# Reordering the first microseconds: a strip's part split around a tile's turns, turns and strip parts exchanged, and PSUM emptied by ScalarE for tiles 0 and 2 and by VectorE for tiles 1 and 3

## The chip, the cores and the metric

The kernel runs on one core of a Trainium2 chip. The metric is the device time of one execution in microseconds (us). The kernel before takes 215.81 us (median of 3 runs, 215.74 to 215.83). The change touches only the first 12 us, in which TensorE waits 0.72 us in all (below), so it can only matter by tenths of a microsecond.

## The reference, cut to what matters

```python
x = A_x                                           # 2048 x 640, bf16
g = sigmoid((x * gate_w).sum(-1, keepdims=True))
a = state_space(x, ...)                           # complex diagonal scan, 640 states
b = gelu(x @ w1 + b1) @ w2 + b2                   # w1: 640 x 1728
out = g * a + (1 - g) * b
```

The change concerns only the start of `x @ w1` for the first 512 rows of x (chunk 0).

## The kernel before, the parts that the change touches

TensorE contracts over partitions, so x is needed transposed, as `xT[0][:, k, row]` with k = 0 to 4 counting 128-wide slices of the 640 columns. The later chunks are transposed by DMA. Chunk 0 is needed first and is handled otherwise: its four 128-row tiles are loaded as they are and each 128x128 block is turned on TensorE by a matmul with the identity. A turn lands in PSUM, and VectorE or ScalarE copies it to `xT`. The loads are issued in pieces, in order of urgency:

```python
    load_x0(nc.sync, 0, 1, 0, KA * P)             # tile 0, k = 0 and 1 (KA = 2)
    load_w1a(nc.scalar, 0)
    load_x0(nc.sync, 1, 2, 0, KA * P)             # tile 1
    load_w1a(nc.scalar, 1)
    load_x0(nc.sync, 2, 3, 0, KA * P)             # tile 2
    load_x0(nc.scalar, 0, H, KA * P, D)           # tiles 0 and 1, k = 2 to 4
    load_x0(nc.sync, 3, 4, 0, KA * P)             # tile 3
    load_w1a(nc.sync, 2)
    # ... (cut)
    rows(nc.sync, prmA[0:KS, :], A_log_dt)        # three small parameter loads
    rows(nc.sync, prmA[KS:2 * KS, :], A_Lambda_im)
    rows(nc.sync, prmA[2 * KS:3 * KS, :], A_Lambda_re)
    load_x0(nc.sync, H, TPC, KA * P, D)           # tiles 2 and 3, k = 2 to 4: "the x load"
    nc.sync.dma_start(out=w1a34[:], ...)          # w1 for k = 3 and 4: "the w1 load"
```

Dummy matmuls keep TensorE busy until the first tile is there. Then turns and useful matmuls alternate:

```python
    pA = bank()
    for n in (512, 512, 512, 512, 512, 128, 128, 128, 128):
        nc.tensor.matmul(pA[:, 0:n], lhsT=ones(P), rhs=ones(n), start=True, stop=True)

    def turn(p, col, a, kd):
        nc.tensor.matmul(p[:, col:col + P], lhsT=xn[0][:, a, kd * P:(kd + 1) * P], rhs=ident[:], start=True, stop=True,
                         skip_group_check=True)

    def turned(engine, p, col, a, k0, k1):
        dst = xT[0][:, k0:k1, a * P:(a + 1) * P]
        src = p[:, col:col + (k1 - k0) * P].rearrange("p (k t) -> p k t", t=P)
        if engine is nc.vector:
            nc.vector.tensor_copy(out=dst, in_=src)
        else:
            nc.scalar.activation(out=dst, in_=src, func=ACT.Identity)

    def turn_first(a, other):
        t = bank()
        turn(t, 0, a, 0)
        turned(nc.vector, t, 0, a, 0, 1)
        turn(other, a * P, a, 1)
        turned(nc.scalar, other, a * P, a, 1, 2)

    turn_first(0, pA)
```

Six PSUM banks hold the first six 128-wide slices of the hidden layer for all 512 rows. `part(k, a)` adds slice k of tile a to all six, in six matmuls of 128 columns. `turn_first` turns k = 0 and 1 of a tile, `turn_rest` k = 2 to 4. All eight banks are in use: six accumulators, `pA`, and one that is handed from `bank()` to `bank()`. A turn into a bank must wait until the earlier turn there has been emptied.

```python
    def strip(kd, t0, t1, first, f0=0, f1=FA):
        for kf in range(f0, f1):
            ff1_mm(banks[kf], 0, kf, kd, t0, t1, first, 3)

    def turn_rest(a, t, *parts):
        for k in range(KA, KD):
            turn(t, (k - KA) * P, a, k)
        for engine, k0, k1 in parts:
            turned(engine, t, (k0 - KA) * P, a, k0, k1)

    # ... (cut: scratch tiles and helpers of the state-space part, such as u, red, ab, FSC and over)
    def part(kd, a):
        strip(kd, a * P, (a + 1) * P, kd == 0)

    for _ in range(3):
        nc.tensor.matmul(banks[0][:, 0:P], lhsT=ones(P), rhs=ones(P), start=True, stop=True, skip_group_check=True)
    part(0, 0)
    turn_first(1, pA)
    part(1, 0)
    turn_first(2, pA)
    part(0, 1)
    part(1, 1)
    turn_first(3, pA)
    part(0, 2)
    part(1, 2)
    nc.tensor.matmul(pA[:, 0:3 * KS], lhsT=prmA[:], rhs=ident[:, 0:3 * KS], start=True, stop=True, skip_group_check=True)
    nc.vector.tensor_copy(out=colA[:], in_=pA[:, 0:3 * KS])
    nc.scalar.activation(out=dt16[:], in_=ldt_c, func=ACT.Exp)
    nc.vector.tensor_scalar(out=limp[:], in0=lim_c, scalar1=INV_2PI, scalar2=None, op0=ALU.mult)
    turn_rest(0, bank(), (nc.scalar, KA, KD))
    part(0, 3)
    nc.vector.tensor_tensor(out=dtl[:], in0=dt16[:], in1=lre_c, op=ALU.mult)
    nc.vector.tensor_tensor(out=thp_c[:], in0=dt16[:], in1=limp[:], op=ALU.mult)
    turn_rest(1, pA, (nc.vector, KA, KD))
    nc.scalar.activation(out=r_c[:], in_=dtl[:], func=ACT.Exp)
    part(1, 3)
    turn_rest(2, bank(), (nc.scalar, KA, KD))
    part(2, 0)
    nc.vector.tensor_tensor(out=u, in0=tf[:].rearrange("p (o i) -> p o i", o=1).to_broadcast([P, KS, NP]), in1=over(thp_c[:], NP), op=ALU.mult)
    turn_rest(3, pA, (nc.scalar, KA + 1, KD), (nc.vector, KA, KA + 1))
    nc.vector.tensor_copy(out=kk[:], in_=u)
    nc.vector.tensor_tensor(out=red, in0=u, in1=kk[:], op=ALU.subtract)
    part(2, 1)
    part(2, 2)
    AHEAD = 3
    strip(KD - 1, 0, HT, False, 0, AHEAD)
    part(2, 3)
    nc.scalar.activation(out=FSC[:, 0:KS, 0:NP], in_=red, func=ACT.Sin, scale=TWO_PI_M)
    nc.vector.scalar_tensor_tensor(out=ab, in0=red, scalar=-1.0, in1=red, op0=ALU.mult, op1=ALU.max)
    nc.scalar.activation(out=FSC[:, KS:2 * KS, 0:NP], in_=ab, func=ACT.Sin, scale=-TWO_PI_M, bias=halfpi[:])
    for kf in range(FA):
        if kf == 3:
            nc.tensor.matmul(pA[:, 0:NB], lhsT=prmB[:], rhs=ident[:, 0:NB], start=True, stop=True, skip_group_check=True)
            nc.vector.tensor_copy(out=colB[:], in_=pA[:, 0:NB])
            for j in range(KD):
                nc.vector.tensor_copy(out=w1c[j][:, n1c - 1:n1c], in_=pA[:, j:j + 1])
        for kd in (4, 3):
            ff1_mm(banks[kf], 0, kf, kd, HT if kd == 4 and kf < AHEAD else 0, CH, False, 3)
    for kf in range(FA):
        ff1_act(banks[kf], 0, kf)
    two_banks = [bank(), bank()]
    for kd in range(KD):
        for i in range(2):
            ff1_mm(two_banks[i], 0, FA + i, kd)
    for i in range(2):
        ff1_act(two_banks[i], 0, FA + i)
    ff1(0, FA + 2)
```

## Time and profile before

| | before |
|---|---|
| time, median of 3 runs | 215.81 us |
| span of the profiled execution | 213.8 us |
| TensorE busy | 209.5 us |
| first useful matmul (first strip) | 4.00 us |
| first matmul with `w1b`, the next columns of w1 (end of the part that the change touches) | 12.51 us |
| second half's x load landed / w1 load for k = 3 and 4 landed | 8.16 / 9.14 us |

These lines are from the page of the kernel before: the span, the busy time of two engines with its share of the span, and the chain of work that ended last, by engine and by line.

```profile
span 213.8 us, 3591 instructions
...
PE 209.5 (98%) x1399; PEld 126.2 (59%) x1410; DVE 189.2 (88%) x387; ACT 103.2 (48%) x186; POOL 1.0 (0%) x13
...
PE 95%; DMA 3%; SPq 0%; issue 0%; DVE 0%
PE bank L607 27%; PE bank L267 25%; PE bank L666 20%; PE bank L548 20%; DMA xn<-in_A_x_dram 2%; DMA w1a<-in_B_w_dram 1%; PE bank L623 1%; PE bank L293 1%; SPq L130 0%; PE bank L233 0%; DVE ot L671 0%; PE bank L283 0%; PE bank L395 0%
```

TensorE is the limit, and 3% of the chain are DMAs, all of them in the first 9 us. The next lines are from the timeline of the kernel before, merged into groups: start, duration, engine, line, operation, out<-in, count, and in brackets the idle time just before with what ended it.

```profile
4.00 0.60 PE L267 MATMUL bank<-xT,w1a 128*128 128x128 bf16 x6
...
4.44 0.28 PE L233 MATMUL bank<-ident,xn 128*128 128x128 bf16 x2
...
4.55 0.50 PE L267 MATMUL bank<-xT,w1a 128*128 128x128 bf16 x6
...
4.70 0.29 DVE L240 CAST xT<-bank 128x128 bf16<-128x128 f32 x1 [0.75 <-PE bank L233]
...
5.04 0.27 PE L233 MATMUL bank<-ident,xn 128*128 128x128 bf16 x2
...
5.94 0.83 PE L267 MATMUL bank<-xT,w1a 128*128 128x128 bf16 x12
...
6.92 0.17 PE L368 MATMUL bank<-ident,prmA 128*128 128x15 bf16 x1 [0.15 <-DMA prmA<-in_A_Lambda_re_dram]
...
7.62 0.50 PE L267 MATMUL bank<-xT,w1a 128*128 128x128 bf16 x6
...
8.20 0.17 PEld L233 LDWEIGHTS <-xn 128*128 128x128 bf16 x3 [0.26 <-DMA xn<-in_A_x_dram]
8.20 0.34 PE L233 MATMUL bank<-ident,xn 128*128 128x128 bf16 x3
...
12.51 0.59 PE L267 MATMUL bank<-xT,w1b 128*128 128x512 bf16 x2
```

A merged TensorE line must be read with care: the end of a matmul is modelled and overlaps the next, so a short wait does not appear as a gap. Read starts instead. A 128-column matmul may follow another after 56 ns, so the six of 4.55 us let the next group start at 4.55 + 6 x 0.056 = 4.89 us; it started at 5.04. The 0.15 us are a wait for the VectorE copy on the line before, which began at 4.70, took 0.29 and freed the bank. In the same way, twelve matmuls from 5.94 end their turn at 6.61, and the parameters' turn (L368) started at 6.92; six from 7.62 end at 7.95, and the rest of tile 2 started at 8.20, where the weight load also shows the wait openly, for the x load. These three waits sum to 0.72 us. When a load has landed is read from the semaphore records in the trace, where each of the large loads counts to 16.

### The profile page before, as it was taken

How to read it: one execution, taken by the hardware profiler on the slowest of the kernel's cores; microseconds unless marked ns; L12 is line 12 of the kernel's file. 1: busy time of each engine (PE TensorE's matmuls, PEld its weight loads, DVE VectorE, ACT ScalarE, POOL GpSimd, SP SyncE). 2: the span in 40 equal slices, each digit the busy share in tenths (PEclk: the TensorE clock that was granted, in tenths of full speed). 3: DMA queues.
4: the chain of work that ended last, by engine and by line, in shares of the span. 5: the costliest groups of instructions: out<-in, count | busy, mean ns of one | idle time of the engine just before them, and what ended most of it. 6: DMA issues, size and time to landing. Idle time of an engine off the chain costs nothing.

```text
span 213.8 us, 3591 instructions
## 1 busy us (share of the span) xinstructions
PE 209.5 (98%) x1399; PEld 126.2 (59%) x1410; DVE 189.2 (88%) x387; ACT 103.2 (48%) x186; POOL 1.0 (0%) x13
## 2 busy tenths in 40 slices
PE   8999999999999999999999999999999999999994
PEld 5845444454476644775457777444457687676774
DVE  2699999999998999999999999999999999993153
ACT  3699856675758588203563210455683422305100
POOL 1000000000000000000000000000000000000000
DMA  6879999997000000051000005100000000100011
GB/s 194 247 162 180 208 175 293 312 214 187 0 0 0 3 0 0 17 175 71 0 0 3 0 0 180 68 0 2 3 0 14 3 0 31 61 34 0 0 66 61
DMA packets 31571, 15.84 MB, mean 74 GB/s; under 512 B 22978, under 2 KB 31554, under 8 KB 31554
## 3 DMA queue, kind: packets, MB, share of 16 engines
q1 hardware_dynamic: 30850, 14.99, 28.9%
q10 hardware_dynamic: 704, 0.62, 0.9%
q8 instruction: 11, 0.18, 0.3%
q14 instruction: 6, 0.05, 0.1%
HBM read 7.48 MB, written 2.62 MB: 47 GB/s over the span
## 4 chain that ended last, share of the span: by engine, by line
PE 95%; DMA 3%; SPq 0%; issue 0%; DVE 0%
PE bank L607 27%; PE bank L267 25%; PE bank L666 20%; PE bank L548 20%; DMA xn<-in_A_x_dram 2%; DMA w1a<-in_B_w_dram 1%; PE bank L623 1%; PE bank L293 1%; SPq L130 0%; PE bank L233 0%; DVE ot L671 0%; PE bank L283 0%; PE bank L395 0%
## 5 line engine op out<-in xcount | busy, mean ns | idle before, releaser
L607 PE MATMUL bank<-w_sb,gel 128*128 128x384 bf16 (+1 forms) x416 | 57.9, 299 | 0.0
L607 PEld LDWEIGHTS <-gel 128*128 128x128 bf16 x416 | 40.3, 98 | 17.0 <-issue 0.8
L551 ACT ACTIVATE bu<-bank 128x512 bf16<-128x512 f32 x40 | 23.7, 598 | 37.6 <-PE bank L548 37.5
L272 ACT ACTIVATE gel<-bank,colB 128x512 bf16<-128x512 f32 x52 | 33.8, 694 | 10.9 <-PE bank L267 10.6
L666 PEld LDWEIGHTS <-hs 128*128 128x128 bf16 x330 | 31.7, 98 | 11.6
L502 DVE TENSOR_TENSOR_SCAN g<-r_c,carry,v 128x512 bf16<-128x512 f32 x30 | 37.2, 1269 | 0.0
L615 ACT ACTIVATE gb<-bank,gcol 128x384 f32<-128x384 f32 (+1 forms) x32 | 15.1, 526 | 33.2 <-PE bank L607 16.8
L267 PE MATMUL bank<-xT,w1a 128*128 128x512 bf16 (+2 forms) x173 | 27.7, 310 | 0.2
L666 PE MATMUL bank<-CT_im,hs 128*128 128x320 bf16 (+2 forms) x165 | 27.1, 295 | 0.0
L666 PE MATMUL bank<-CT_re,hs 128*128 128x320 bf16 (+2 forms) x165 | 27.1, 295 | 0.0
L671 DVE SCALAR_TENSOR_TENSOR ot<-bank,gcol,gb 128x320 bf16<-128x320 f32 (+2 forms) x33 | 17.4, 532 | 10.0 <-PE bank L666 9.5
L548 PE MATMUL bank<-xT,BT_im 128*128 128x512 bf16 x99 | 24.8, 379 | 0.1
L548 PE MATMUL bank<-xT,BT_re 128*128 128x512 bf16 x97 | 24.5, 379 | 0.2
L267 PEld LDWEIGHTS <-w1a 128*128 128x128 bf16 x177 | 14.6, 98 | 11.5
L267 PE MATMUL bank<-xT,w1b 128*128 128x512 bf16 x80 | 17.9, 379 | 0.0
L548 PEld LDWEIGHTS <-BT_im 128*128 128x128 bf16 x100 | 9.8, 98 | 11.8
L581 DVE TENSOR_TENSOR bank<-xn,Dbc 128x320 f32<-128x320 bf16 (+2 forms) x33 | 14.5, 482 | 2.0 <-ACT gb L615 2.0
L548 PEld LDWEIGHTS <-BT_re 128*128 128x128 bf16 x100 | 9.7, 98 | 11.0
L483 DVE TENSOR_TENSOR v<-wa,wb 128x512 bf16<-128x512 bf16 x40 | 15.2, 420 | 0.6
L596 ACT ACTIVATE bank<-b2bc 128x384 f32<-128x384 bf16 (+1 forms) x24 | 11.7, 526 | 7.6 <-DVE ot L671 7.6
L483 DVE TENSOR_TENSOR wa<-TCOS,g 128x1024 bf16<-128x1024 bf16 x20 | 13.7, 685 | 0.1
L267 PE MATMUL bank<-xT,w1c 128*128 128x512 bf16 x57 | 13.6, 379 | 0.2
(99 smaller groups left out, 166.0 us busy)
## 6 DMA issues: line engine op xcount, KB each, us to landing
out_dram<-ot SPq DMA_DIRECT2D x15, 160.0 KB, 1.8
w_sb<-in_B_w_dram SPq DMA_DIRECT2D x1, 2080.0 KB
xn<-in_A_x_dram SPq DMA_DIRECT2D x3, 640.0 KB
w1b<-in_B_w_dram SPq DMA_DIRECT2D x5, 128.0 KB, 3.6
w1c<-in_B_w_dram SPq DMA_DIRECT2D x5, 112.0 KB, 2.7
w1a<-in_B_w_dram ACTq DMA_DIRECT2D x2, 192.0 KB, 3.1
w1a<-in_B_w_dram SPq DMA_DIRECT2D x1, 384.0 KB, 4.1
xn<-in_A_x_dram SPq DMA_DIRECT2D x4, 64.0 KB, 2.9
```

The source lines that it names most:

```text
L267: nc.tensor.matmul(p[:, t0:t1], lhsT=w, rhs=xT[c][:, kd, t0:t1], start=(kd == 0) if first is None else first, stop=(kd == last), skip_grou ...
L272: nc.scalar.activation(out=gel[c][:, kf, :], in_=p[:, :], func=ACT.Gelu_apprx_tanh, bias=b1_c[:, kf:kf + 1])
L483: nc.vector.tensor_tensor(out=o, in0=a, in1=b, op=op)
L502: nc.vector.tensor_tensor_scan(s["g"][:, ri, :], r_c[:, ks:ks + 1].to_broadcast([P, CH]), s["v"][:, ri, :], init, ALU.mult, ALU.add)
L548: nc.tensor.matmul(p[:], lhsT=BT[ks >= KSA][:, kd, (ks % KSA if ks < KSA else ks - KSA) * P:][:, 0:P], rhs=xT[c][:, kd, :], start=(kd == 0 ...
L551: nc.scalar.activation(out=bu[:, ri, :], in_=p[:], func=ACT.Identity)
L581: dve_now(ck.pe, 0.45, lambda: nc.vector.tensor_tensor(out=p[:, 0:d1 - d0], in0=xn[c][:, a, d0:d1], in1=Dbc[:, d0:d1], op=ALU.mult))
L596: nc.scalar.activation(out=v, in_=src, func=ACT.Identity)
L607: nc.tensor.matmul(p[:, col:col + d1 - d0], lhsT=gel[c][:, kf, a * P:(a + 1) * P], rhs=w2_sb[:, kf, d0:d1], start=False, stop=False, skip_ ...
L615: nc.scalar.activation(out=gbs[ti][:, d0:d1], in_=p[:, col:col + d1 - d0], func=ACT.Identity, scale=gcol[:, 1, ti:ti + 1])
L666: nc.tensor.matmul(p[:, 0:d1 - d0], lhsT=hs[c][:, j, lo:lo + P], rhs=CT[:, j % KS, d0:d1], start=False, stop=(j == 2 * KS - 1), skip_group ...
L671: nc.vector.scalar_tensor_tensor(out=ot[:, d0:d1], in0=p[:, 0:d1 - d0], scalar=gcol[:, 0, ti:ti + 1], in1=gbs[ti][:, d0:d1], op0=ALU.mult, ...
```

## The change

The intent is to fill these waits. Tile 1's turns start in the middle of tile 0's first part, so that its copy is ready earlier; tile 0's rest is turned ahead of the parameters; the turns that need the x load move behind `part(2, 0)` and `part(2, 1)`; ScalarE empties the rest of tiles 0 and 2 and VectorE that of tiles 1 and 3 (new for tile 3 only, which the two had shared), and the k = 4 strip for the first 256 columns is done for all six banks and earlier.

```diff
--- before.py
+++ after.py
@@ -356,8 +356,9 @@
 
     for _ in range(3):
         nc.tensor.matmul(banks[0][:, 0:P], lhsT=ones(P), rhs=ones(P), start=True, stop=True, skip_group_check=True)
-    part(0, 0)
+    strip(0, 0, P, True, 0, FA // 2)
     turn_first(1, pA)
+    strip(0, 0, P, True, FA // 2, FA)
     part(1, 0)
     turn_first(2, pA)
     part(0, 1)
@@ -365,27 +366,27 @@
     turn_first(3, pA)
     part(0, 2)
     part(1, 2)
-    nc.tensor.matmul(pA[:, 0:3 * KS], lhsT=prmA[:], rhs=ident[:, 0:3 * KS], start=True, stop=True, skip_group_check=True)
-    nc.vector.tensor_copy(out=colA[:], in_=pA[:, 0:3 * KS])
+    turn_rest(0, pA, (nc.scalar, KA, KD))
+    pP = bank()
+    nc.tensor.matmul(pP[:, 0:3 * KS], lhsT=prmA[:], rhs=ident[:, 0:3 * KS], start=True, stop=True, skip_group_check=True)
+    nc.vector.tensor_copy(out=colA[:], in_=pP[:, 0:3 * KS])
     nc.scalar.activation(out=dt16[:], in_=ldt_c, func=ACT.Exp)
     nc.vector.tensor_scalar(out=limp[:], in0=lim_c, scalar1=INV_2PI, scalar2=None, op0=ALU.mult)
-    turn_rest(0, bank(), (nc.scalar, KA, KD))
     part(0, 3)
+    turn_rest(1, bank(), (nc.vector, KA, KD))
     nc.vector.tensor_tensor(out=dtl[:], in0=dt16[:], in1=lre_c, op=ALU.mult)
     nc.vector.tensor_tensor(out=thp_c[:], in0=dt16[:], in1=limp[:], op=ALU.mult)
-    turn_rest(1, pA, (nc.vector, KA, KD))
     nc.scalar.activation(out=r_c[:], in_=dtl[:], func=ACT.Exp)
+    nc.vector.tensor_tensor(out=u, in0=tf[:].rearrange("p (o i) -> p o i", o=1).to_broadcast([P, KS, NP]), in1=over(thp_c[:], NP), op=ALU.mult)
     part(1, 3)
-    turn_rest(2, bank(), (nc.scalar, KA, KD))
     part(2, 0)
-    nc.vector.tensor_tensor(out=u, in0=tf[:].rearrange("p (o i) -> p o i", o=1).to_broadcast([P, KS, NP]), in1=over(thp_c[:], NP), op=ALU.mult)
-    turn_rest(3, pA, (nc.scalar, KA + 1, KD), (nc.vector, KA, KA + 1))
+    part(2, 1)
+    turn_rest(2, pA, (nc.scalar, KA, KD))
+    turn_rest(3, bank(), (nc.vector, KA, KD))
     nc.vector.tensor_copy(out=kk[:], in_=u)
     nc.vector.tensor_tensor(out=red, in0=u, in1=kk[:], op=ALU.subtract)
-    part(2, 1)
+    strip(KD - 1, 0, HT, False)
     part(2, 2)
-    AHEAD = 3
-    strip(KD - 1, 0, HT, False, 0, AHEAD)
     part(2, 3)
     nc.scalar.activation(out=FSC[:, 0:KS, 0:NP], in_=red, func=ACT.Sin, scale=TWO_PI_M)
     nc.vector.scalar_tensor_tensor(out=ab, in0=red, scalar=-1.0, in1=red, op0=ALU.mult, op1=ALU.max)
@@ -397,7 +398,7 @@
             for j in range(KD):
                 nc.vector.tensor_copy(out=w1c[j][:, n1c - 1:n1c], in_=pA[:, j:j + 1])
         for kd in (4, 3):
-            ff1_mm(banks[kf], 0, kf, kd, HT if kd == 4 and kf < AHEAD else 0, CH, False, 3)
+            ff1_mm(banks[kf], 0, kf, kd, HT if kd == 4 else 0, CH, False, 3)
     for kf in range(FA):
         ff1_act(banks[kf], 0, kf)
     two_banks = [bank(), bank()]
```

## The prediction

> **What bounds the kernel now.** TensorE: the busy table gives it 209.5 of 213.8 us, the chain of waits 95%. Measuring from matmul start to matmul start, I find no stall after 12.5 us; all the rest is streaming (a 128-column matmul every 56 ns, 256 every 109 ns, 512 every 216 ns, as "TensorE: Matmul & The Clock Gate", Back-to-back issue gap, states for a warm array: N/2.4 + 2.5 ns). So any time saved before 12.5 us passes whole to the end, and nothing else can be saved. Between the first real matmul (4.00) and 12.5 us TensorE stalls three times, 0.72 us in all (timeline):
> - 0.15 us at 5.04: tile 2's turn waits for VectorE to empty tile 1's turn (same bank);
> - 0.31 us at 6.92: the parameter turn waits for its three small loads, the last landing at 6.79;
> - 0.25 us at 8.20: tile 2's rest waits for the x load that lands at 8.16.
>
> **What changes.** Columns streamed are equal; three wide matmuls become six halves (~8 ns). Tile 1's turns start three strip matmuls earlier; tile 0's rest moves ahead of the parameter turn; tiles 2 and 3's rest moves behind parts (2,0) and (2,1); the whole 256-column strip of k=4 moves ahead of parts (2,2) and (2,3). Replay with the durations and landings of the trace:
> - Tile 1's turn at 4.28 instead of 4.44. VectorE's copy (0.29) ends near 4.83, so the 0.15 us stall goes. But tile 3's x lands at 5.77 and its turn already started at 5.82 without slack: the 0.15 us comes back as a wait there.
> - 6.61: tile 0's rest (0.17) fills part of the parameter wait; parameters still at 6.92. Gain 0.17.
> - Tile 1's rest now shares a bank with the parameters and waits for VectorE's copy of them (ends 7.30): +0.06.
> - Part (2,1) now comes right after (2,0) and needs tile 1's rest, emptied by VectorE in 0.56 us (about 7.72 to 8.28): starts 8.33, +0.14.
> - The x load of 8.16 is no longer waited for. Both rests end at 9.00. The k=4 strip then needs the w1 load that lands at 9.14: starts about 9.19, +0.19. Before it was needed at 9.50.
> - From there 6x109 + 12x56 + 6x325 + 30 ns = 3.30 us: end near 12.49 against 12.51.
>
> So stalls of about 0.70 us replace 0.72: the kernel swaps a wait for x at 8.16 with 4.31 us of work behind it for a wait for w1 at 9.14 with 3.30 us behind it. If landings are earlier without the profiler, both chains shorten about equally; perhaps 0.1 to 0.2 us more for the new one if w1's last piece comes early. That is likely: 15 of its 16 semaphore steps are there at 8.41, the last comes 0.73 us later ("DMA: Bandwidth & Descriptors", Why a DMA increments its semaphore by 16: only the full 16 means all data landed; this trace agrees). ScalarE and VectorE move by at most 0.1 us, and the activations' banks have about 0.9 us of slack at 14.7.
>
> **Time.** 215.7 us, 215.35 to 215.95 eight times in ten. Faster by over 2%: 1%; within 2%: 98%; slower by over 2%: 1%.
>
> **Right or wrong in the profile.** No gap before tile 2's turn; a gap to about 5.82 before tile 3's; parameters at 6.92; small gaps before tile 1's rest and part (2,1); k=4 strip starting 0.05 us after its load lands; first w1b matmul at 12.3 to 12.55; everything after it unchanged but shifted.
>
> **What would make it wrong.** Loads landing at other times (x of tile 3, parameters, last w1 piece), which now decide more; a stall on VectorE before part (2,1) longer than 0.2 us; a different chip.

## The result, and the profile after

| | before | after |
|---|---|---|
| time, median of 6 runs | 215.82 us (215.72 to 215.97) | 215.87 us (215.40 to 216.01) |
| span of the profiled execution | 213.8 us | 214.1 us |
| first strip matmul | 4.00 us | 3.97 us |
| first `w1b` matmul | 12.51 us | 12.80 us |
| from the first `w1b` matmul to the last matmul | 198.33 us | 198.33 us |

The ratio of times is 0.9998, with a 95% interval of 0.9985 to 1.0010: the same. Ratios and intervals here are not quite the ratio of the medians. "The same", "faster" and "slower" are judged at 2%.

The same lines of the page, for the kernel after:

```profile
span 214.1 us, 3607 instructions
...
PE 210.6 (98%) x1413; PEld 127.4 (59%) x1413; DVE 189.1 (88%) x387; ACT 102.7 (48%) x185; POOL 1.0 (0%) x13
...
PE 98%; DVE 0%; issue 0%
PE bank L267 27%; PE bank L608 27%; PE bank L667 20%; PE bank L549 20%; PE bank L230 1%; PE bank L624 1%; PE bank L293 1%; PE bank L233 1%; DVE ot L672 0%; PE bank L358 0%; PE bank L283 0%; PE bank L396 0%; PE bank L371 0%
```

The DMAs have left the chain that ended last: no wait for a load is left on it. Still the first `w1b` matmul came 0.29 us later. The timeline of the kernel after (columns as before) shows why:

```profile
3.97 0.48 PE L267 MATMUL bank<-xT,w1a 128*128 128x128 bf16 x3
...
4.25 0.42 PE L233 MATMUL bank<-ident,xn 128*128 128x128 bf16 x2
...
4.46 1.16 PE L267 MATMUL bank<-xT,w1a 128*128 128x128 bf16 x9
...
5.42 0.42 PE L233 MATMUL bank<-ident,xn 128*128 128x128 bf16 x2
...
7.42 0.49 PE L267 MATMUL bank<-xT,w1a 128*128 128x128 bf16 x6
...
7.63 0.17 DVE L372 COPY colA<-bank 128x15 f32<-128x15 f32 x1 [0.64 <-PE bank L371]
...
7.86 0.33 PE L233 MATMUL bank<-ident,xn 128*128 128x128 bf16 x3
...
8.02 1.30 PE L267 MATMUL bank<-xT,w1a 128*128 128x128 bf16 x18
8.22 0.56 DVE L240 CAST xT<-bank 128x384 bf16<-128x384 f32 x1 [0.21 <-PE bank L233]
...
9.50 2.46 PE L267 MATMUL bank<-xT,w1a 128*128 128x256 bf16 x24
...
12.80 0.38 PE L267 MATMUL bank<-xT,w1b 128*128 128x512 bf16 x1
```

Look at the starts first. The three matmuls of 3.97 are followed at 4.25, not at 3.97 + 3 x 0.056 = 4.14. Nine from 4.46 reach to 5.42, which is 107 ns each. So TensorE still ran at half rate, and it did until 5.92 us, where the trace has the clock record that grants full rate. I call this moment the release of the clock. In the profile of before the 107 ns spacing ended at 4.27 us: the group after the six matmuls of 4.00 started at 4.44, only 0.10 us later than 4.00 + 6 x 0.056. After that the line reads as predicted at two places: six matmuls from 7.42 could end at 7.76, but tile 1's rest starts at 7.86 (0.10 us, for VectorE's copy of the parameters at 7.63, which share its bank); in the 18 matmuls from 8.02 hides a wait of 0.14 us, before the first of `part(2, 1)` at 8.83, for the copy of 0.56 us that VectorE began at 8.22. No other wait is left.

The time from the first strip matmul to the first `w1b` matmul can now be taken apart. Without any wait and at full rate it is 7.67 us in either kernel (worked out below, from runs at full rate without waits for loads, less their engine waits). I add the waits (excess of the distance between two starts over N/2.4 + 2.5 ns, with N columns) and the excess of the half-rate matmuls:

| profile | streaming | waits | half rate | sum | measured |
|---|---|---|---|---|---|
| before | 7.67 | 0.72 | 0.10 | 8.49 | 8.51 |
| after | 7.67 | 0.24 | 0.90 | 8.81 | 8.83 |

So in this pair the change took out 0.48 us of waiting, and a later release of the clock put in 0.80 us. The question for the experiments is whether the second has anything to do with the change, and what the change is worth without it.

Theory A: the moment of release varies from run to run whatever the kernel; the change exchanges waits for loads, which vanish by themselves when TensorE is late, for waits for VectorE, which don't. Theory B: the change itself delays the release. Theory C: the change costs some 0.3 us in any case.

### The profile page after: what moved, and what is told of

It reads as the page before. It is cut to its first block, busy times and chain, and to the rows that moved or that the text cites. A ratio compares the mean times of both kernels' runs of the same rounds, so it can differ in the third digit from the quotient of the medians.

```text
span 214.1 us, 3607 instructions
## 1 busy us (share of the span) xinstructions
PE 210.6 (98%) x1413; PEld 127.4 (59%) x1413; DVE 189.1 (88%) x387; ACT 102.7 (48%) x185; POOL 1.0 (0%) x13
## 4 chain that ended last, share of the span: by engine, by line
PE 98%; DVE 0%; issue 0%
PE bank L267 27%; PE bank L608 27%; PE bank L667 20%; PE bank L549 20%; PE bank L230 1%; PE bank L624 1%; PE bank L293 1%; PE bank L233 1%; DVE ot L672 0%; PE bank L358 0%; PE bank L283 0%; PE bank L396 0%; PE bank L371 0%
## 5 line engine op out<-in xcount | busy, mean ns | idle before, releaser
L267 PE MATMUL bank<-xT,w1a 128*128 128x512 bf16 (+2 forms) x180 | 28.6, 315 | 0.0
L267 PEld LDWEIGHTS <-w1a 128*128 128x128 bf16 x180 | 15.5, 102 | 11.3
```

What stands on the lines that cost most here:

```text
L267: nc.tensor.matmul(p[:, t0:t1], lhsT=w, rhs=xT[c][:, kd, t0:t1], start=(kd == 0) if first is None else first, stop=(kd == last), skip_grou ...
```

## The experiments

All results below were correct. Those of experiments 2, 3 and 5 and fill_both_landed are single executions, whose state is unknown (granted clock 0.999 to 1.0); of them only times within the profile are used.

### 1. Both kernels again: `before_again`, `after_again`, `after_third`

No edit. Expected of before_again:

> The kernel before, unchanged, run again. Theory A (the array's clock is released at a moment that varies from run to run, whatever the kernel): the half-rate spacing of 107 ns between 128-column matmuls ends anywhere between about 4.2 us (seen in the first profile of before) and about 7 us, and if late, the waits for loads shrink: the wait of 0.25 us for the x load goes to about 0.17 us or less, and the first w1b matmul starts at about 12.65 to 12.75 instead of 12.51. Theory B (the change itself delays the release): the release is at 4.2 us again and the first w1b matmul at 12.5. Ratio to before 1.000.

Of after_again:

> The changed kernel, unchanged, run again. Theory A: the release time is again a lottery; if it comes near 4.2 us, the first w1b matmul starts at about 12.42 to 12.50 with waits for tile 3's x load and for the w1 load as predicted; if it comes near 5.9 us, at about 12.80 with only the two VectorE waits (0.10 and 0.14 us) that the first profile of after shows. Theory B: release at 5.9 us again. Theory C (the change really costs 0.3 us): 12.8 whatever the release. Ratio to before 0.999 to 1.001 under A.

Of after_third:

> The changed kernel a third time, because the five runs of after_again (215.04 to 216.24) lay 0.2% above before. Theory A (the moment at which the array's clock is released and the landings of the loads vary from run to run; the change itself is worth between -0.05 and +0.12 us): single runs between 215.0 and 216.3, ratio to before between 0.999 and 1.002, and not always on the same side. Theory C (the change costs 0.3 to 0.5 us): ratio 1.0015 to 1.003 again.

| profile | full rate from | x load landed | w1 load landed | waits | first `w1b` | span |
|---|---|---|---|---|---|---|
| before | 4.27 | 8.16 | 9.14 | 0.72 | 12.51 | 213.8 |
| before_again | 4.25 | 6.98 | 8.34 | 0.20 | 11.95 | 213.2 |
| after | 5.92 | 7.29 | 8.91 | 0.24 | 12.80 | 214.1 |
| after_again | 3.98 or earlier | 7.08 | 8.34 | 0.28 | 11.94 | 213.2 |
| after_third | 3.80 | 7.83 | 8.81 | 0.50 | 12.16 | 213.5 |

"Full rate from" is the clock record where a trace has one, and else the end of the 107 ns spacing. Timeline of before_again, TensorE alone:

```profile
3.97 0.61 PE L267 MATMUL bank<-xT,w1a 128*128 128x128 bf16 x6
4.42 0.28 PE L233 MATMUL bank<-ident,xn 128*128 128x128 bf16 x2
...
11.95 1.03 PE L267 MATMUL bank<-xT,w1b 128*128 128x512 bf16 x4
```

The same of after_again:

```profile
3.98 0.33 PE L267 MATMUL bank<-xT,w1a 128*128 128x128 bf16 x3
4.14 0.27 PE L233 MATMUL bank<-ident,xn 128*128 128x128 bf16 x2
...
11.94 1.03 PE L267 MATMUL bank<-xT,w1b 128*128 128x512 bf16 x4
```

Theory B and the strict form of theory C fall: the changed kernel gets its full rate at 3.8 us as well as at 5.9, and with early clock and punctual loads the first `w1b` matmuls of the two kernels are 0.01 us apart (11.95 and 11.94). This is not yet equality at the same clock: before_again still has 0.10 us of half rate behind its first strip matmul, and after_again has none. Without that the changed kernel is about 0.09 us behind, an estimate from these two profiles: it has the two VectorE waits of 0.24 us and one of 0.04 us for tile 2's x load, against 0.20 us of engine waits. Both expectations put the first `w1b` matmul near 12.4 us or later and missed, since the loads landed earlier than in the profile that I had replayed. The two VectorE waits of the changed kernel are in all three of its profiles, each time 0.10 and 0.14 us. In after_third there is besides a wait of 0.25 us before tile 2's turn, not for VectorE, but for tile 2's x load, which landed at 4.96 us.

The timed rounds are less kind. Against before of the same rounds, before_again has a ratio of 0.9993 (0.9980 to 1.0006), after_again 1.0022 (1.0008 to 1.0036) and after_third 1.0019 (1.0003 to 1.0034). The ratio of after_again lies above the range that I had given for theory A (0.999 to 1.001), and that of after_third fits theory A (up to 1.002) and theory C (from 1.0015) alike, so the timed runs don't decide between them. My expectation that the changed kernel would not always be on the same side failed for the two later comparisons. These ratios are not quotients of plain means: dividing the means gives 1.0010 and 1.0012, that is 0.22 and 0.25 us. All fast runs of the timed rounds together: before, 30 runs, mean 215.68 us, standard deviation 0.24; after, 17 runs, mean 215.87 us, standard deviation 0.39. The difference of 0.19 us has a standard error of 0.10 (worked out from these figures; one run of before at 277.71 us, with a granted clock of 0.756, is left out). These runs come from several sessions, the two later ones on different chips, so this is a rough figure. The profiled run of after_again and that of after_third are each the lowest of their set (215.04 and 215.26 us). Five of the other nine have spans of 214.4 to 214.7 us, longer than any profile of the changed kernel above (213.2 to 214.1 us), so what took the time in these runs is not seen.

### 2. Loads and clock taken out: `before_landed`, `after_landed`

```diff
-    for n in (512, 512, 512, 512, 512, 128, 128, 128, 128):
+    for n in (512,) * 36 + (128, 128, 128, 128):
```

With 31 more dummy matmuls of 512 columns, the first useful matmul starts at 11.50 us (before) and 11.62 us (after), when all loads of this stage are in and the clock is released (at 4.95 and 5.21 us). Expected:

> The kernel before with 36 instead of 5 wide dummy matmuls ahead, so that every load of the first stage has landed and the clock is released before the first real matmul. What is left are waits for VectorE and ScalarE. Estimate by replaying the order of before with the durations of its trace: waits of 0.15 us before tile 2's turn and 0.17 us before tile 2's rest (bank emptied by ScalarE), none for a load; from the first strip matmul to the first w1b matmul 7.96 us (it was 8.51 in the first profile). A rival that holds the loads for innocent expects 8.4 or more.

> The changed kernel with the same 36 dummy matmuls. Replay: no wait before tile 2's turn, 0.10 to 0.14 us before tile 1's rest, 0.14 us before part (2,1), none for a load; from the first strip matmul to the first w1b matmul 7.92 us, so 0.04 us less than before_landed: the change swaps engine waits of 0.32 us for engine waits of 0.28 us. If the change removed waits for good, the difference would be 0.15 us or more; if it cost, after_landed would be longer.

Measured from the first strip matmul to the first `w1b` matmul: 7.87 us before, 7.91 us after. Timeline of before_landed, TensorE alone, columns as before:

```profile
11.50 0.49 PE L267 MATMUL bank<-xT,w1a 128*128 128x128 bf16 x6 [0.15 <-DVE xT L240]
...
11.94 0.50 PE L267 MATMUL bank<-xT,w1a 128*128 128x128 bf16 x6
12.43 0.27 PE L233 MATMUL bank<-ident,xn 128*128 128x128 bf16 x2
...
19.37 1.03 PE L267 MATMUL bank<-xT,w1b 128*128 128x512 bf16 x4
```

Six matmuls from 11.94 could end at 12.28; tile 2's turn started at 12.43: the wait of 0.155 us for VectorE, unchanged. There is one more, of 0.05 us, before tile 2's rest, where I had expected 0.17. Timeline of after_landed, TensorE alone:

```profile
11.62 0.33 PE L267 MATMUL bank<-xT,w1a 128*128 128x128 bf16 x3 [0.15 <-DVE xT L240]
...
14.16 0.49 PE L267 MATMUL bank<-xT,w1a 128*128 128x128 bf16 x6
14.59 0.33 PE L233 MATMUL bank<-ident,xn 128*128 128x128 bf16 x3
14.76 1.31 PE L267 MATMUL bank<-xT,w1a 128*128 128x128 bf16 x18
15.90 0.50 PE L233 MATMUL bank<-ident,xn 128*128 128x128 bf16 x6
...
19.54 1.03 PE L267 MATMUL bank<-xT,w1b 128*128 128x512 bf16 x4
```

The six matmuls from 14.16 could end at 14.49, and tile 1's rest came at 14.59; the 18 from 14.76 take 1.14 us to the next start instead of 1.00. These are the waits of 0.10 and 0.14 us. So before has 0.20 us of engine waits and after 0.24 us, and the rest is 7.67 us in both. With loads and clock out of the way, the change is worth nothing: it is 0.05 us longer, where I had expected 0.04 us shorter, mainly because I had put the 0.05 us wait of before at 0.17.

### 3. The first step alone: `split_only_landed`

This is the kernel before with the 36 dummies and only this edit:

```diff
-    part(0, 0)
+    strip(0, 0, P, True, 0, FA // 2)
     turn_first(1, pA)
+    strip(0, 0, P, True, FA // 2, FA)
     part(1, 0)
```

> The kernel before plus only the split of the first strip's part around tile 1's turns, with the 36 dummy matmuls that take loads and clock out. The wait of 0.155 us before tile 2's turn goes and nothing comes back: first strip matmul to first w1b matmul 7.71 us, against 7.87 (before_landed) and 7.91 (after_landed). If the split only moves the wait to another instruction even with the loads there, it stays at 7.87.

Measured: 7.71 us, as expected. The wait before tile 2's turn is gone and nothing comes back. The split is the part of the change that is good: it saves 0.155 us when loads are in, and the reordering behind it gives back 0.20 us (7.91 against 7.71). There was no run for the split alone with real loads, so its time is open, and so is whether the wait would come back there for tile 3's x load, as I had predicted. The exchange of engines for tile 3's rest was not run alone either.

### 4. The two new waits filled: `fill_both_landed`, `fill_both`

The changed kernel, with tile 1's rest turned two matmuls later and tile 2's rest moved between the two parts:

```diff
     part(0, 3)
+    strip(1, 3 * P, 4 * P, False, 0, 2)
     turn_rest(1, bank(), (nc.vector, KA, KD))
     ...
-    part(1, 3)
+    strip(1, 3 * P, 4 * P, False, 2, FA)
     part(2, 0)
-    part(2, 1)
     turn_rest(2, pA, (nc.scalar, KA, KD))
+    part(2, 1)
     turn_rest(3, bank(), (nc.vector, KA, KD))
```

> The kernel of fill_both with the 36 dummy matmuls. Waits of 0.101 and 0.142 us of after_landed fall to under 0.1 us together: first strip matmul to first w1b matmul 7.67 to 7.78 us, against 7.91 in after_landed. If the two waits are not what the reordering cost, it stays at 7.91.

> The changed kernel with its two new VectorE waits filled: tile 1's rest turns two strip matmuls later, tile 2's rest turns move between parts (2,0) and (2,1). Theory A: in the profile the waits of 0.10 and 0.14 us shrink to under 0.1 us together; the time from the first strip matmul to the first w1b matmul is 0.1 to 0.2 us under that of the changed kernel at the same release of the clock, unless the w1 load lands after 9.0 us and takes it back; ratio to before 0.998 to 1.001, too small to be clear of the scatter. A rival that holds the order of turns for harmless expects no difference in the profile.

With the dummies it takes 7.76 us, as expected, 0.15 us less than after_landed. Timeline of fill_both_landed, TensorE alone:

```profile
11.87 0.33 PE L267 MATMUL bank<-xT,w1a 128*128 128x128 bf16 x3 [0.15 <-DVE xT L240]
...
15.58 0.33 PE L233 MATMUL bank<-ident,xn 128*128 128x128 bf16 x3
15.83 0.49 PE L267 MATMUL bank<-xT,w1a 128*128 128x128 bf16 x6
...
19.63 0.81 PE L267 MATMUL bank<-xT,w1b 128*128 128x512 bf16 x3
```

Three turns from 15.58 could end at 15.75, and `part(2, 1)` started at 15.83: of the two waits, 0.09 us is left at one place. With real loads, the profile of fill_both (full rate from 5.22 us) has this one wait of 0.09 us and no other, and the first `w1b` matmul at 12.31 us. From the first strip matmul that is 7.67 + 0.09 + 0.57 for half rate = 8.33 us, and 8.34 were measured.

Six timed runs lie between 214.85 and 215.39 us, median 215.26; the ratio to before is 0.9978 (0.9964 to 0.9991), a little below the range that I had expected (0.998 to 1.001) and, against my expectation, clear of the scatter. This kernel is faster than before by more than the scatter, though far less than 2%, and it is the only version here that beats both. The size is larger than the waits explain: the interval begins at 0.09% (0.2 us), while the engine waits account for 0.12 us with an early clock (0.20 in before_again, 0.09 here) and for nothing with a late one (0.05 us in before_w1_late, below). What the rest is stays open.

### 5. Which load decides: `before_x_last`, `after_x_last`, `before_w1_late`, `after_w1_late`

In the first pair two issues are exchanged, so that the x load lands after the w1 load:

```diff
-    load_x0(nc.sync, H, TPC, KA * P, D)
     nc.sync.dma_start(out=w1a34[:], ...)
+    load_x0(nc.sync, H, TPC, KA * P, D)
```

> The kernel before with the issue order of two loads exchanged: the w1 load for k=3 and 4 first, then the second half's x load, which so lands at about 8.3 to 9.2 us instead of 7.0 to 8.2. The theory (the kernel before hangs on this x load with 4.31 us of streaming behind it): tile 2's rest starts 0.05 us after the landing, and the first w1b matmul starts 4.31 to 4.35 us after the landing, at about 12.7 to 13.5. Rival (loads do not decide): start at 11.95 to 12.75 as before.

> The changed kernel with the same exchange. The theory: it reaches that load two parts later, so behind it lie 3.64 us of streaming (turns of both rests, strip, two parts, loop); if the x load lands after TensorE arrives (about 8.1 early clock, 9.1 late clock), the first w1b matmul starts about 3.65 us after the landing, 0.65 us earlier relative to the landing than in before_x_last; if it lands before, no wait for it and 11.9 to 12.8. So with this order the change should gain up to 0.6 us.

In the second pair an unused load delays the w1 load:

```diff
+    junk = const.tile([P, 1024], BF16, name="junk")
+    nc.sync.dma_start(out=junk[:], in_=B_w1[0:P, 0:1024])
     nc.sync.dma_start(out=w1a34[:], ...)
```

> The kernel before with an unused 256 KB load ahead of the w1 load for k=3 and 4, which so lands at about 9.1 to 10.1 us instead of 8.3 to 9.1. The theory: behind this load before has about 3.0 us of streaming (three half strips, part (2,3), loop), so it waits only where the landing comes after about 8.9 (early clock) or 9.7 (late clock); first w1b matmul at the landing plus about 3.0 us, or 11.95 to 12.75 without a wait.

> The changed kernel with the same extra load. The theory: behind the w1 load lie 3.30 us of streaming, so the first w1b matmul starts about 3.35 us after the landing if TensorE waits for it (arrival at about 8.7 early clock, 9.5 late clock), 0.3 us later relative to the landing than before: with this load late the change loses up to 0.3 us. Rival (loads do not decide): no wait before the k=4 strip.

| profile | full rate from | x load landed | w1 load landed | wait for the late load | first `w1b` | after that landing |
|---|---|---|---|---|---|---|
| before_x_last | 4.69 | 8.51 | 8.02 | 0.62 | 12.86 | 4.35 |
| after_x_last | 6.38 | 8.33 | 7.83 | none | 13.02 | (not waited for) |
| before_w1_late | 6.34 | 7.23 | 10.00 | 0.07 | 13.02 | 3.02 |
| after_w1_late | 3.88 | 7.10 | 9.72 | 0.98 | 13.07 | 3.35 |

Timeline of before_x_last, weight loads (PEld) and TensorE:

```profile
7.61 0.50 PE L267 MATMUL bank<-xT,w1a 128*128 128x128 bf16 x6
...
8.55 0.17 PEld L233 LDWEIGHTS <-xn 128*128 128x128 bf16 x3 [0.62 <-DMA xn<-in_A_x_dram]
...
12.86 0.59 PE L267 MATMUL bank<-xT,w1b 128*128 128x512 bf16 x2
```

The weight load for tile 2's rest is issued 0.04 us after the x load landed, and from the landing to the `w1b` matmul it takes 4.35 us. Timeline of after_w1_late (the two added lines of code move line numbers by two):

```profile
8.44 0.50 PE L235 MATMUL bank<-ident,xn 128*128 128x128 bf16 x6
...
9.76 2.09 PEld L269 LDWEIGHTS <-w1a 128*128 128x128 bf16 x24 [0.99 <-DMA w1a<-in_B_w_dram]
...
13.07 0.38 PE L269 MATMUL bank<-xT,w1b 128*128 128x512 bf16 x1
```

Here the k = 4 strip waits 0.98 us for the w1 load, and 3.35 us lie behind it. So the exchange that I had predicted is shown in its parts: behind the x load before has 4.35 us of work; behind the w1 load before has 3.02 and after 3.35 us. after_w1_late also shows the wait for tile 3's x load: it landed at 5.67 us, and the turn was 0.11 us late, at 5.71.

after_x_last missed. I had allowed for a gain of up to 0.6 us, and it came 0.16 us after before_x_last: the clock was released only at 6.38 us, TensorE came to the x load at 9.39 us, a full microsecond after its landing, and had no wait to save. The pair thus does not measure the gain. It gives something else: with before_w1_late, two profiles with almost the same late release (6.34 and 6.38 us). Timeline of before_w1_late, TensorE:

```profile
5.03 0.84 PE L269 MATMUL bank<-xT,w1a 128*128 128x128 bf16 x6
...
5.67 0.42 PE L235 MATMUL bank<-ident,xn 128*128 128x128 bf16 x2
...
8.26 0.50 PE L269 MATMUL bank<-xT,w1a 128*128 128x128 bf16 x6
...
8.64 0.33 PE L235 MATMUL bank<-ident,xn 128*128 128x128 bf16 x3
```

Six matmuls from 5.03 take 6 x 0.107 = 0.64 us, and tile 2's turn follows at 5.67 without a wait: at half rate the copy of tile 1 is ready in time without any split. So before has only the engine wait of 0.05 us before tile 2's rest at 8.64 (and the artificial 0.07 us for the load); after has 0.10 + 0.14 us. With a late clock the change therefore costs about 0.2 us, an estimate from the waits of these two profiles, and it has nothing to give for it.

## Why the prediction was right, and where it was not

**Total.** 215.7 us was predicted (215.35 to 215.95), and the median was 215.87. That the number hit is in part luck. In the profile the first `w1b` matmul came at 12.80 us, outside the predicted 12.3 to 12.55; of the five waits that the replay left, only the two for VectorE occurred there (those for tile 3's x load, the parameters and the w1 load did not), and a late clock more than made up for them. The range of 0.6 us is about as wide as the scatter of the six runs of after (215.40 to 216.01), two of which lie above it. The core of the argument holds: only what happens before the first `w1b` matmul counts. From there to the last matmul it took 198.33 us in all of the 14 profiles, with a spread of 10 ns. And the change does exchange one set of waits for another of like size.

**The wait before tile 2's turn goes.** Right: split_only_landed takes out exactly 0.155 us.

**It comes back as a wait for tile 3's x load.** In the profile of after it did not, since TensorE was late and the load was in (5.74 us). It is seen in after_w1_late, with 0.11 us. In after_third it was tile 2's load instead, with 0.25 us. So the step holds only in some executions.

**Two new waits for VectorE, 0.06 and 0.14 us.** Right in kind; measured 0.10 and 0.14 us in every profile of the changed order. The first was sized too low by 0.04 us.

**The parameters' wait shrinks to 0.14 us.** It was gone in every profile of the changed order, and in before_again too: the last of the three small loads landed at 6.80 us in after and at 6.14 in after_again, and their turn came at 7.40 and 6.54.

**A wait of 0.19 us for the w1 load.** It did not occur in the profile of after (landed at 8.91, needed at 9.50), nor in after_again (landed at 8.34), and in after_third the landing at 8.81 just coincided with the start at 8.85. The mechanism is real (after_w1_late: 0.98 us of wait and 3.35 us behind it, against 3.30 predicted), but the loads were mostly earlier than in the one profile I replayed.

**A term was missing: the clock.** I took the release at about 4.2 us in the profile of before as a constant. It lies between 3.7 and 6.4 us in the 14 profiles, on both sides for both orders, and in the profile of after it cost 0.80 us more than in that of before. It also decides what the change is worth. With an early clock the loads bind and the waits for them are hidden or not by luck (0.72 us of waits in one profile of before, 0.20 us in another). With a late clock TensorE arrives after the loads, their waits vanish, and what stays are the engine waits, of which the changed order has more: 0.24 us against 0.05 us (after_x_last and before_w1_late, one profile of each order). This is shown for the profiles. For the timed runs it is only the likely reason why those of after scatter wider (0.39 against 0.24 us standard deviation) and lie on average 0.19 us higher: the direction and size agree with 0.05 us (landed) and 0.2 us (late clock), but the release is not recorded for each timed run. That the recorded ratios of the two later comparisons amount to 0.4 to 0.5 us is not settled. The small extra gain that I had allowed for from an early last piece of w1 is not seen in any comparison.

## What to carry to other kernels

A wait for a load and a wait for another engine are not of the same kind. Here a late clock absorbed the waits for loads, and of the engine waits only the one before tile 2's turn (0.15 us in before, none in before_w1_late); the two new ones of the changed order, 0.10 and 0.14 us, stayed in all six of its profiles. So an exchange of one kind for the other can look even in a replay of one trace and still lose. Before reordering, find out which of the two each gap is, and after it look for dependences that have become adjacent, here a part placed too soon behind the copy that it needs; two small moves of independent work into the gaps gave back 0.15 us (7.91 to 7.76). And before comparing two profiles that differ by tenths of a microsecond, look at where the array's half-rate spacing ends in each.

## What the Trainium skill lacked or had wrong

- "TensorE: Matmul & The Clock Gate", What's actually happening: it says that the window of about 3.4 us is free-running and that the transition varies by about 500 ns either way; a note there adds that one kernel showed 6, 11 or 14 slow matmuls. The runs agree that it varies, but more widely than 500 ns: full rate from 3.7 to 6.4 us in 14 profiles whose matmuls all begin at 0.8 us. The same note puts the penalty below 1% of a typical span and advises against fitting a particular count. The 0.80 us between the two first profiles are 0.4% of the span, which agrees, but for a kernel tuned to tenths of a microsecond they are the largest difference between these two.
- The same page, Back-to-back issue gap: it gives N/2.4 + 2.5 ns for an isolated matmul, and for a stream of pairs of weight load and matmul about 81 ns at 128 columns and 131 ns at 512. The stream here is made of such pairs (24 weight loads for the 24 matmuls from 9.76 us in after_w1_late), and still its spacing at full rate is that of the first formula: 56, 109 and 216 ns for 128, 256 and 512 columns (and 107 ns for 128 at half rate).
- "DMA: Bandwidth & Descriptors", Why a DMA increments its semaphore by 16 and not by 1: only the full count means that all data have landed, and here the reader started only after it (tile 2's rest in before at 8.20 us, with the 15th step at 7.17 and the 16th at 8.16). It gives no figure for how far the last step lags behind the fifteenth: here, for the same x load in different executions, 0.99 us (7.17 to 8.16), 0.73 us (7.10 to 7.83), 0.23 us (7.06 to 7.29) and 0.06 us (6.92 to 6.98).
- No page that I read says that the same exchange of waits can be worth a gain or a loss by the phase of the clock; the numbers are 0.20 against 0.24 us of engine waits with the clock released, and 0.05 against 0.24 us with a late release.
